# Attention and a gated MLP on one core: products taken bank by bank, low halves of the weights in eight 256-KB slots

## The chip, the core and the metric

The kernel runs on one core of a Trainium2 chip. The metric is the device time of one execution in microseconds. Engines are named as in the profile: PE (TensorE), DVE (VectorE), ACT (ScalarE), POOL (GpSimd) and SP, whose queue issues every DMA.

## What is computed

Banded attention with sinks over 4 batches of 8 heads, 768 positions of 64 columns, then a gated MLP over the 3072 tokens that come out:

```python
keep = is_sink | in_window                      # 4 sinks, a window of 128
a = softmax(where(keep, q @ k.T / 8, -1e9))
x = (a @ v).transpose(0, 2, 1, 3).reshape(3072, 512)
gate = 1.0 / (1.0 + np.exp(-(x @ w_gate)))      # 512 x 1536
val = x @ w_val                                 # 512 x 1536
out = gate * val @ w_out                        # 1536 x 512
```

The weights come as 64-bit floats and are decoded on the chip.

## The kernel before

**Work.** The tokens are twelve groups of 256 (tn 0 to 11, three per batch). `attend` makes one unit of attention, a head of a group. `CHUNKS` joins the groups to nine chunks for the MLP: 0 to 4 and 8 are one group each, 5 to 7 are pairs of two. d_ff is cut into NF = 12 slices f of 128. For each chunk and slice the MLP multiplies the transposed x by the slice's gate and value columns into PSUM banks m0 and m1 (`B_m` = 2), forms (1 + tanh) * value in `th` with `cv` as a side store, splits it into gh and gl, and multiplies by the slice's rows of w_out into output banks (the downs).

**Precision.** From chunk 1 on every product is three fp32r matmuls: high half by high, high by low, low by high. `product` is one such product of two 128-row steps, six matmuls of 256 columns. High halves of the weights stay in SBUF (`ws`, 68 slots), low halves are written to `wlo_d` in DRAM (`spare`) and streamed back for each chunk and slice by `fetch`. Chunk 0 runs in plain fp32 (`feed_whole`).

**Plain chunks** (`feed_plain`): the value matrix had the gate matrix subtracted in its first half (`halves`), so a slice is four products, all in one bank: g0, v0, v2, then g2 on top of g0; a copy of g0's part in between and an addition afterwards make the value. 24 matmuls of 256 columns and 6 of 512.

**Pairs** (`feed_pair`) use seven products instead of eight for two groups, with sums of x made by `second_half` and of the weights by `thirds`: 42 matmuls of 256 columns and 12 of 512 per slice. Two of the four output banks come from the tag "a", of which attention has the rest (`B_a` = 3; o0, o1 and o2 are banks of their own).

**Order.** `Plan` gets every operation with a priority, the engines that may take it, what it reads and writes (a tile, or one part of it) and a duration, runs a list schedule over them with modelled times, and emits the instructions in the order that comes out; each engine then keeps that order. Attention ranks by its unit number ahead of the MLP's PE work (10000 + chunk), while the MLP's ACT and DVE work ranks first (-1000 + chunk). What waits for what on the chip is set by the framework below, from the tiles that an instruction touches. Where PE has nothing early on, the plan puts a warm-up matmul (`warm`) into its order.

**Loads.** Pieces of `wlo_d` go into three slots of 512 KB (`wst`, shared with the decoding of the weights, in pool p2) and two of 256 KB (`wol`). A pair's slice loads two of 512 KB and one of 256, a plain slice one of each.

Of the kernel before, what the change touches and what calls it, by code (L numbers as in the profile page):

```python
# [24 lines left out]
CHUNKS = ((0,), (1,), (2,), (3,), (4,), (5, 6), (7, 8), (9, 10), (11,))  # L25
NWS = 68
# [7 lines left out]
HALVED = 30000.0  # L34
CROWDED = 350000.0
# [10 lines left out]
KS1 = 14.0  # L46
# [32 lines left out]
B_wol = 2  # L79
B_w2 = 2  # L80
B_wst = 3
B_a = 3
# [14 lines left out]
def general(ctx, tc, qk, v, ident, nsk, win, wres, wlo_d, out):  # L97
# [34 lines left out]
    with tc.For_i(0, B, 1) as b:  # L132
# [65 lines left out]
        with tc.For_i(0, NT, 1) as t:  # L198
# [18 lines left out]
            for f in range(NF):  # L217
                wgh, wvh, woh = wres[f]
                lows = []
                for i, n in ((1, "g"), (2, "v"), (4, "o")):  # L220
# [6 lines left out]
                for nm in "gv":  # L227
                    m = ps.tile([128, 128], F32, name="m" + nm)
                    ms.append(m)
                    g, v2 = (wgh, wgl), (wvh, wvl)  # L230
                    terms = (
                        [(c, g) for c in range(NC)] if nm == "g"
                        else [(c, g) for c in range(NC // 2)] + [(c, v2) for c in range(NC)]
                    )
                    todo = [
                        (c, w, x) for c, (wh, wl) in terms
                        for w, x in ((wh, xh), (wh, xl), (wl, xh))
                    ]
# [60 lines left out]
class Op:  # L299
    def __init__(self, prio, ways, dma, busy):  # L300
        self.prio, self.ways, self.dma, self.busy = prio, ways, dma, busy
        self.after, self.before, self.tiles = [], 0, []
# [3 lines left out]
class Plan:  # L306
# [9 lines left out]
    def op(self, prio, ways, r=(), w=(), dma=0.0, busy=0.97, start=0.0):  # L316
        o = Op(prio, ways, dma, busy)
        o.ready = start
        seen = set()
# [21 lines left out]
    def run(self, warm, fill_ns, fill):  # L341
# [35 lines left out]
        while events:  # L377
# [25 lines left out]
            for e in free:  # L403
# [4 lines left out]
                while waiting[e] or unsure:  # L408
# [66 lines left out]
                    heapq.heappush(events, (end, n, ("end", o, e)))  # L475
                    for x in o.after:
# [25 lines left out]
def kernel(  # L502
# [31 lines left out]
    p2 = main.enter_context(tc.tile_pool(name="p2", bufs=1))  # L534
    ps = main.enter_context(tc.tile_pool(name="ps", bufs=1, space=PSUM))

# [35 lines left out]
    def dma(prio, ns, fn, r=(), w=(), start=0.0):  # L572
        plan.op(prio, [("Q", ISSUE, fn)], r, w, dma=ns, start=start)
# [158 lines left out]
    idle = ps.tile([128, 512], F32, tag="o20", name="idle")  # L732
    PE.matmul(idle[:, 0:128], lhsT=ident, rhs=ident, start=True, stop=True)

    def warm():
        PE.matmul(
            idle[:, 0:128], lhsT=ident, rhs=ident, start=False, stop=True,
# [11 lines left out]
    pair_of = {x: len(parts) > 1 for parts in CHUNKS for x in parts}  # L749
# [17 lines left out]
    WLO, LOADS, GROUPS, DECODED, READY = (Fixed(None) for _ in range(5))  # L767

    def sinks(b, u):
# [21 lines left out]
        for o in range(0, 128, NS):  # L791
# [3 lines left out]
                ), [], [(raw, o)] + [VSHL[b, i] for i in range(2) if (b, i) in VSHL],  # L795
            )
        for i in range(0 if b else 1, 2):
# [3 lines left out]
            copy(u, H // 2 * D, hi, x, [raw], [both])  # L801
# [18 lines left out]
    def attend(u, b, h, t0, T, XR):  # L820
# [296 lines left out]
        if y:  # L1117
# [8 lines left out]
            elif not pair_of[tn]:  # L1126
                if c % 2 == 0:
                    for x in XH, XL:
                        x[tn, c // 2] = tile([128, 2, W], F32R, "ws", NWS, wp)
                H1, L1 = XH[tn, c // 2], XL[tn, c // 2]  # L1130
                hi, lo = lambda: H1()[:, c % 2], lambda: L1()[:, c % 2]
                copy(u, W, hi, xv, read, [(H1, c)], plain)
                rest(u, W, lo, xv, hi, read + [(H1, c)], [(L1, c)], plain)
# [7 lines left out]
    def minus(p, cols, out, a, b, r, w, add=False):  # L1141
# [7 lines left out]
            ], r, w,  # L1149
# [24 lines left out]
    wlo_d = dram.tile([NF, 128, 5 * 512], F32, name="wlo_d")  # L1174
# [79 lines left out]
    def halves(f):  # L1254
# [3 lines left out]
        woh = halve(pr, f, 4, (1, DO), wout, (), HALVED)  # L1258
        minus(
            pr, 256, lambda: value()[:, 0:2], lambda: value()[:, 0:2], lambda: gate()[:, 0:2],  # L1260
            [gate], [value],
        )
        gh = halve(pr, f, 1, (NC, 128), gate)
        vh = halve(pr, f, 2, (NC, 128), value)
        wres[f] = [gh, vh, woh]

    def thirds(f):
# [3 lines left out]
        t2 = lambda: value()[:, 2:4]  # L1271
        minus(pr, 256, t2, t2, lambda: value()[:, 0:2], [], [value])
        minus(pr, 256, lambda: gate()[:, 0:2], t2, lambda: gate()[:, 0:2], [value], [gate])
        minus(pr, 256, lambda: gate()[:, 2:4], lambda: gate()[:, 2:4], t2, [value], [gate])
        both = slot(F32R, (NC, 128))
        copy(pr, 256, lambda: both()[:, 0:2], t2, [value], [(both, 0)])
        rest(pr, 256, lambda: both()[:, 2:4], t2, lambda: both()[:, 0:2], [value, (both, 0)], [(both, 1)])
        spare(pr, f, 0, both)
        wres[f].append(halve(pr, f, 3, (NC, 128), gate))
# [15 lines left out]
    def feed(ci):  # L1295
# [4 lines left out]
            tile([128, DO], F32, f"o{j}", 1, ps) if j < 3  # L1300
            else tile([128, DO], F32, "a", BUFS["a"], ps) for j in range(T)
        ]
        for f in range(NF):
# [3 lines left out]
            elif T == 2:  # L1307
                feed_plain(ci, tcs[0], f, O)
# [55 lines left out]
    def fetch(pr, f, k, n, chain, gate=()):  # L1364
        x = (
            tile([128, n * 512], F32R, "wst", BUFS["wst"], p2) if n > 1
            else tile([128, 512], F32R, "wol", BUFS["wol"])
        )
        dma(
            pr, 728.0 * n, lambda: Q.dma_start(  # L1370
                out=x().bitcast(F32), in_=wlo_d[f, :, k * 512 : (k + n) * 512]
            ), [(WLO, (f, k + i)) for i in range(n)] + list(gate), [x, (LOADS, chain)],
        )
        return x

    def product(p, m, reg, w, c0, w2, d0, X, first, last, w_):

        XHn, XLn = X

        def go():  # L1380
            for i in range(2):
                hi, lo = w(c0 + i), w2(d0 + i)
                for k, (a, x) in enumerate(((hi, XHn), (hi, XLn), (lo, XHn))):
                    PE.matmul(
                        m()[:, reg * 256 : reg * 256 + 256], lhsT=a, rhs=x()[:, i],
# [4 lines left out]
        plan.op(p, [("PE", 6 * mac(256), go)], w_[0] + [XHn, XLn], w_[1])  # L1390

    def gated(pr, W, th, cv, step):

        gh = tile([128, W], F32R, "gh", BUFS["gh"])
        gl = tile([128, W], F32R, "gl", BUFS["gl"])
        n = W // 256
        t, c = (lambda x=x: x()[:, 0:n].rearrange("p n x -> p (n x)") for x in (th, cv))
        plan.op(
            pr, [("V", vec(W), lambda: V.scalar_tensor_tensor(
                out=t(), in0=t(), scalar=1.0, in1=c(), op0=ALU.add, op1=ALU.mult  # L1400
            ))],
            [cv], [th],
        )
# [22 lines left out]
    def feed_plain(ci, n, f, O):  # L1426
        pr = -1000.0 + ci + f / NF
        pe = 10000.0 + ci + f / NF
        gh_, vh_, woh = wres[f][:3]
        e = fetch(pr, f, 1, 2, 0, [DECODED] if ci == WHOLE else ())  # L1430
        wol = fetch(pr, f, 4, 1, 1, [DECODED] if ci == WHOLE else ())
        m = Tile(MS, None, F32, "m", BUFS["m"])
        th = tile([128, 2, 256], F32, "th", BUFS["th"])
        cv = tile([128, 2, 256], F32, "cv", BUFS["cv"])
        A1, A2 = (XH[n, 0], XL[n, 0]), (XH[n, 1], XL[n, 1])
        gw, vw = (lambda i: gh_()[:, i]), (lambda i: vh_()[:, i])
        product(pe, m, 0, gw, 0, four(e), 0, A1, True, False, ([gh_, e], [m, GROUPS]))
# [172 lines left out]
```

## Time and profile before

| | us |
|---|---|
| median of 3 runs | 856.19 (855.15 to 857.5) |
| the profiled execution | 857.94 |
| its span, first to last instruction | 855.8 |
| PE busy | 787.8 (92%), 5110 matmuls |
| DVE busy | 656.1 (77%) |
| POOL busy | 527.6 (62%) |
| ACT busy | 442.8 (52%) |
| DMA | 172.97 MB, queue 1 at 65.9% of the 16 engines |

The granted clock of PE is 0.989 over the span. The waits in the profile are the idle time of an engine just ahead of an instruction, put down to what released it. Chunk 0 ends near 157 us, chunk 4 near 434, the pairs near 565, 690 and 794; the last scores of attention are done at 704 us.

### The profile page before, as it was taken

What the parts mean: (1) busy time and instruction counts of PE and PEld (TensorE: products, weight loads), DVE (VectorE), ACT (ScalarE), POOL (GpSimd) and SP (SyncE); (2) the same over time, 40 slices, a digit from 0 to 9 for tenths busy, and PEclk for the clock granted to TensorE, in tenths of its full rate; (3) what the DMA queues carried; (4) which work ended last, traced back from release to release, by engine and by line L of the source; (5) the groups of instructions that cost most, each with busy time, mean ns of one, the idle gap of its engine ahead of it and who ended that gap; (6) DMA issues with size and microseconds to landing.
All of it is one profiled execution on the core that took longest, in us unless ns stands there. A gap on an engine that the chain in (4) does not pass through costs nothing. (4 is left out here: it accounts for less than half of the span.)

```text
span 855.8 us, 16414 instructions
## 1 busy us (share of the span) xinstructions
PE 787.8 (92%) x5110; PEld 697.1 (81%) x5110; DVE 656.1 (77%) x1871; ACT 442.8 (52%) x1288; POOL 527.6 (62%) x698
## 2 busy tenths in 40 slices
PE   7999988887999999999899999999999899999995
PEld 6777766786888898889788889898888788888884
DVE  6899999898798988738888988878887986444221
ACT  7788776552566666626565554454545661001111
POOL 4899897675667786627778678657675872111111
PEclk9999999899999999999999999999999999999998
DMA  6889887788776676667666656666665554545651
GB/s 175 230 258 294 287 261 233 235 292 286 222 224 194 205 237 181 203 201 225 185 194 192 182 169 192 184 221 194 196 194 177 142 179 139 162 148 162 196 178 55
DMA packets 111341, 172.97 MB, mean 202 GB/s; under 512 B 46480, under 2 KB 58768, under 8 KB 111248
## 3 DMA queue, kind: packets, MB, share of 16 engines
q1 hardware_dynamic: 111248, 171.86, 65.9%
q8 instruction: 43, 0.70, 0.3%
q14 instruction: 50, 0.41, 0.2%
HBM read 149.80 MB, written 22.02 MB: 201 GB/s over the span
## 5 line engine op out<-in xcount | busy, mean ns | idle before, releaser
L554 PE MATMUL m<-ws,ws 128*128 128x256 f32 x1824 | 353.8, 290 | 38.8 <-DVE cv L554 29.3
L554 PEld LDWEIGHTS m<-ws,ws 128*128 128x128 f32 x1824 | 286.3, 190 | 64.9 <-DVE cv L554 45.0
L554 PE MATMUL m<-ws,wst 128*128 128x256 f32 x1128 | 286.1, 283 | 2.4 <-DVE cv L554 1.4
L554 PEld LDWEIGHTS m<-ws,wst 128*128 128x128 f32 x1128 | 200.3, 190 | 4.1 <-ACT cv L554 1.9
L554 POOL TENSOR_TENSOR gl<-th,gh 128x256 fp32r<-128x256 f32 (+1 forms) x60 | 58.9, 982 | 142.6 <-DVE gh L554 77.3
L554 POOL TENSOR_SCALAR_AFFINE_SELECT wt<-wt 128x512 fp32r<-128x512 f32 (+3 forms) x192 | 122.7, 639 | 35.8 <-DVE wt L554 23.8
L554 DVE TENSOR_TENSOR cv<-m,cv 128x256 f32<-128x256 f32 x204 | 85.7, 420 | 65.1 <-PE m L554 58.3
L554 ACT ACTIVATE th<-m 128x256 f32<-128x256 f32 x108 | 41.6, 385 | 148.6 <-PE m L554 110.3
L554 PE MATMUL o<-ws,gh 128*128 128x512 f32 x228 | 91.9, 403 | 0.9 <-ACT w L554 0.5
L554 ACT ACTIVATE P<-P,negm_all 128x144 f32<-128x144 f32 x192 | 79.0, 412 | 23.9 <-DVE negm_all L554 22.2
L554 PE MATMUL o<-ws,gl 128*128 128x512 f32 x228 | 89.7, 394 | 0.2 <-POOLq L1564 0.2
L554 PE MATMUL o<-wol,gh 128*128 128x512 f32 x228 | 89.3, 392 | 0.0
L554 DVE SCALAR_TENSOR_TENSOR th<-th,cv 128x256 f32<-128x256 f32 (+1 forms) x96 | 61.8, 644 | 28.2 <-ACT th L554 26.0
L554 POOL TENSOR_TENSOR ws<-ws,ws 128x512 fp32r<-128x512 f32 (+2 forms) x54 | 66.2, 1239 | 12.4 <-DVE ws L554 3.5
L554 PE MATMUL a<-wt,vhl 128*128 128x256 f32 (+2 forms) x282 | 61.2, 328 | 2.8 <-DVE negm_all L554 2.2
L554 DVE CUSTOM_DVE_ANT_0 P<-a,am 128x144 f32<-128x144 f32 x192 | 58.6, 305 | 6.5 <-PE a L554 0.3
L554 POOL TENSOR_TENSOR hi<-qkT,hi 64x256 fp32r<-64x256 f32 x61 | 48.2, 790 | 16.6 <-issue 5.0
L554 PEld LDWEIGHTS a<-wt,vhl 128*128 128x128 f32 x282 | 48.1, 192 | 9.8 <-issue 2.9
L554 POOL TENSOR_TENSOR kl<-qkT,hi 128x400 fp32r<-128x400 f32 (+1 forms) x48 | 50.8, 1058 | 2.1
L554 PEld LDWEIGHTS o<-ws,gl 128*128 128x128 f32 x228 | 42.9, 188 | 10.7 <-POOLq L1564 0.6
L554 POOL TENSOR_TENSOR sk<-turned,own 128x256 fp32r<-128x256 f32 x46 | 31.4, 683 | 28.2 <-DVE turned L554 19.3
L554 ACT CAST hi<-qkT 128x656 fp32r<-128x656 f32 (+1 forms) x59 | 41.3, 701 | 13.3 <-PE a L554 12.0
(141 smaller groups left out, 1647.5 us busy)
## 6 DMA issues: line engine op xcount, KB each, us to landing
wst<-wlo_d SPq DMA_DIRECT2D x132, 512.0 KB, 3.8
wol<-wlo_d SPq DMA_DIRECT2D x96, 256.0 KB, 3.6
qkT<-in_qk_dram SPq DMA_DIRECT2D x52, 328.0 KB, 3.9
wlo_d<-ws SPq DMA_DIRECT2D x60, 256.0 KB, 3.8
qkT<-in_qk_dram SPq DMA_DIRECT2D x24, 264.0 KB, 3.4
wst<-in_moe_w_gate_dram SPq DMA_DIRECT2D x12, 512.0 KB, 5.1
wst<-in_moe_w_val_dram SPq DMA_DIRECT2D x12, 512.0 KB, 5.0
wst<-in_moe_w_out_dram SPq DMA_DIRECT2D x12, 512.0 KB, 5.0
```

The lines of the kernel that those rows point to most:

```text
L554: return lambda *a, **kw: tc.keep_in_program_order(op(*a, **kw))
```

## The change

A pair's seven products are ordered so that both halves of one bank are written in turn before the other bank is, and every reader is declared to read the whole bank. Plain chunks take the unmodified gate and value matrices: four products, gate into one bank, value into the other, no copy and no addition. The subtraction of the gate moves from `halves` to `thirds`, and `thirds` starts no earlier than 250 us. Low halves come as pieces of 256 KB in eight slots `lo` (a new pool, opened when p2 has been closed) and are issued in one chain. o2 goes, and attention's tag "a" has four banks. The warm-up matmul writes into a corner of m0.

```diff
-KS1 = 14.0
+KS1 = 16.0
+THIRDS = 250000.0
-B_wol = 2
+B_lo = 8
-B_a = 3
+B_a = 4
...
-    idle = ps.tile([128, 512], F32, tag="o20", name="idle")
-    PE.matmul(idle[:, 0:128], lhsT=ident, rhs=ident, start=True, stop=True)
+    PE.matmul(MS[0][:, 384:512], lhsT=ident, rhs=ident, start=True, stop=True)
...
-    wlo_d = dram.tile([NF, 128, 5 * 512], F32, name="wlo_d")
+    wlo_d = dram.tile([NF, 128, 6 * 512], F32, name="wlo_d")
...
     def halves(f):
-        woh = halve(pr, f, 4, (1, DO), wout, (), HALVED)
-        minus(
-            pr, 256, lambda: value()[:, 0:2], lambda: value()[:, 0:2], lambda: gate()[:, 0:2],
-            [gate], [value],
-        )
-        gh = halve(pr, f, 1, (NC, 128), gate)
-        vh = halve(pr, f, 2, (NC, 128), value)
+        woh = halve(pr, f, 5, (1, DO), wout, (), HALVED)
+        gh = halve(pr, f, 3, (NC, 128), gate)
+        vh = halve(pr, f, 4, (NC, 128), value)
...
     def thirds(f):
+        minus(pr, 256, t1, t1, g1, [gate], [value], start=THIRDS + 5000.0 * f)
+        minus(pr, 256, t2, t2, t1, [], [value])
+        minus(pr, 256, g1, t2, g1, [value], [gate])
+        minus(pr, 256, g2, g2, t2, [value], [gate])
+        hi = halve(pr, f, 1, (NC, 128), value)
+        spare(pr, f, 0, hi)
+        wres[f].append(halve(pr, f, 2, (NC, 128), gate))
...
-            tile([128, DO], F32, f"o{j}", 1, ps) if j < 3
+            tile([128, DO], F32, f"o{j}", 1, ps) if j < 2
...
+    def fetch(pr, f, *parts):
+        got = []
+        for k in parts:
+            x = tile([128, 512], F32R, "lo", BUFS["lo"], p3)
+            LAST[0] = dma(
+                pr, 728.0, lambda x=x, k=k: Q.dma_start(
+                    out=x().bitcast(F32), in_=wlo_d[f, :, k * 512 : k * 512 + 512]
+                ), [(WLO, (f, k)), DECODED], [x], behind=LAST[0],
+            )
+            got.append(x)
+        return got
...
     def feed_plain(ci, tcs, f, O):
+        glo, vlo, wol = fetch(pr, f, 3, 4, 5)
+        for i, (hi, lo) in enumerate(((gh_, glo), (vh_, vlo))):
+            m = Tile(MS, None, F32, "m", BUFS["m"])
+            for j in range(2):
+                product(
+                    pe + 0.3 * i / NF, m, 0, W, w, 2 * j, four(lo), 2 * j, cols(j), j == 0, j == 1,
+                    [hi, lo] + both(j), [m] if j else [m, GROUPS] + ([th] if i == 0 else []),
+                )
...
     def feed_pair(ci, tcs, f, O):
-        e = fetch(pr, f, 0, 2, 0)
-        l = fetch(pr, f, 2, 2, 0)
-        wol = fetch(pr, f, 4, 1, 1)
+        t12h, t12l, glo, tlo, vlo, wol = fetch(pr, f, 0, 1, 3, 2, 4, 5)
...
+        product(pe, ma, 0, 256, gw, 0, four(glo), 0, X(n, 0), True, False, [gh_, glo] + xs(n, 0), [ma, GROUPS])
         product(
+            pe + 0.05 / NF, ma, 1, 256, four(t12h), 2, four(t12l), 2, X(k, "s2"), False, True,
...
+            pe + 0.2 / NF, mb, 0, 256, tw, 0, four(tlo), 0, X(k, "s3"), True, False, [th_, tlo] + xs(k, "s3"),
...
+            pe + 0.25 / NF, mb, 1, 256, four(t12h), 0, four(t12l), 0, X(k, "s1"), False, False,
...
+            pe + 0.4 / NF, ma, 0, 256, gw, 2, four(glo), 2, X(n, 1), False, True, [gh_, glo] + xs(n, 1), [ma],
...
+            pe + 0.45 / NF, ma, 1, 256, tw, 2, four(tlo), 2, X(k, 1), True, True,
...
+            pe + 0.6 / NF, mb, 1, 256, vw, 2, four(vlo), 2, X(k, "s4"), False, True,
...
+        downs(pe, f, O, gh, gl, woh, wol, (1.3, 1.5, 1.65, 1.7))
```

PE's order in the third pair, where no attention is left. m_89 and m_90 are the two banks, ws the resident halves and sums of x, wst and lo the streamed pieces. Before, from the end of a slice's second product to the start of the fourth:

```order
L554 MATMUL m_89<-ws_9393,wst_10569 128x256
L554 MATMUL m_90<-ws_9398,ws_2447 128x256 [waits DVE_49]
L554 MATMUL m_90<-ws_9425,ws_2447 128x256
L554 MATMUL m_90<-ws_9398,wst_10606 128x256 [waits DMAHW1_49]
L554 MATMUL m_90<-ws_9398,ws_2447 128x256
L554 MATMUL m_90<-ws_9425,ws_2447 128x256
L554 MATMUL m_90<-ws_9398,wst_10606 128x256
L554 MATMUL m_89<-ws_8477,ws_1562 128x256 [waits DVE_49]
```

Between two writes of bank m_89 with a reader in between stands one product in the other bank. The same place after the change, the last matmul of the third product, the fourth, one down and the first of the fifth:

```order
L575 MATMUL m_90<-ws_9645,lo_10622 128x256
L575 MATMUL m_90<-ws_9649,lo_10575 128x256
L575 MATMUL m_90<-ws_9688,lo_10575 128x256
L575 MATMUL m_90<-ws_9649,lo_10603 128x256
L575 MATMUL m_90<-ws_9649,lo_10575 128x256
L575 MATMUL m_90<-ws_9688,lo_10575 128x256
L575 MATMUL m_90<-ws_9649,lo_10603 128x256
L575 MATMUL o_9985<-ws_1346,gh_10654 128x512 [waits DVE_49]
L575 MATMUL o_9985<-lo_10560,gh_10654 128x512 [waits DMAHW0_49]
L575 MATMUL o_9985<-ws_1346,gl_10664 128x512 [waits Pool_49]
L575 MATMUL m_89<-ws_8418,ws_1561 128x256 [waits DVE_49]
```

The third and fourth products both go to m_90, and with the down they stand between the second product and the next write of m_89.

PE's order in the last chunk, a plain one. Before, the second product of a slice and the start of its third, all in one bank:

```order
L554 MATMUL m_90<-ws_9589,ws_1080 128x256
L554 MATMUL m_90<-ws_9611,ws_1080 128x256
L554 MATMUL m_90<-ws_9589,wst_10853 128x256
L554 MATMUL m_90<-ws_9589,ws_1080 128x256
L554 MATMUL m_90<-ws_9611,ws_1080 128x256
L554 MATMUL m_90<-ws_9589,wst_10853 128x256
L554 MATMUL m_90<-ws_9995,ws_1080 128x256 [waits DVE_49]
```

The third product waits for DVE with nothing in between. After the change, the end of a slice's value product, the downs of the slice before and the start of the next gate product:

```order
L575 MATMUL m_90<-ws_10014,lo_11193 128x256
L575 MATMUL o_10976<-ws_1196,gh_11269 128x512 [waits DVE_49]
L575 MATMUL o_10976<-lo_11166,gh_11269 128x512 [waits DMAHW6_49]
L575 MATMUL o_10976<-ws_1196,gl_11271 128x512 [waits Pool_49]
L575 MATMUL o_10983<-ws_1196,gh_11269 128x512
L575 MATMUL o_10983<-lo_11166,gh_11269 128x512
L575 MATMUL o_10983<-ws_1196,gl_11271 128x512
L575 MATMUL m_89<-ws_9686,ws_1561 128x256 [waits Activation_49]
```

The gate's bank is written again after the whole value product and the downs.

SP's order in the third pair, before and after, some one and a half slices each:

```order
L554 DMA wst_10372<-wlo_d 128x1024 [waits DMAHW3_49,PE_49]
L554 DMA wst_10405<-wlo_d 128x1024 [waits DMAHW5_49,PE_49]
L554 DMA wol_10409<-wlo_d 128x512 [waits DMAHW4_49,PE_49]
L554 DMA wst_10447<-wlo_d 128x1024 [waits DMAHW6_49,PE_49]
L554 DMA wol_10482<-wlo_d 128x512 [waits DMAHW7_49,PE_49]
```

```order
L575 DMA lo_10603<-wlo_d 128x512 [waits DMAHW3_49,DMAHW2_49,PE_49]
L575 DMA lo_10608<-wlo_d 128x512 [waits DMAHW4_49,PE_49]
L575 DMA lo_10622<-wlo_d 128x512 [waits DMAHW5_49,PE_49]
L575 DMA lo_10627<-wlo_d 128x512 [waits DMAHW6_49,PE_49]
L575 DMA lo_10641<-wlo_d 128x512 [waits DMAHW7_49,PE_49]
L575 DMA lo_10656<-wlo_d 128x512 [waits PE_49]
```

Each load waits for PE's last use of its slot; a slice has six of them where it had three.

## Rows read from the trace of the kernel before

**Rows 1.** Busy time by stage: PE, PEld, DVE, ACT, POOL, clock, DMA share, GB/s
```profile
0.00:139.00 139.00, 124.63 (x619) 96.19 (x620) 126.45 (x325) 107.25 (x260) 112.72 (x135) 0.99 0.82 246
139.00:226.00 87.00, 73.54 (x478) 65.05 (x478) 73.95 (x172) 42.13 (x121) 57.14 (x71) 0.96 0.80 259
226.00:434.00 208.00, 197.68 (x1366) 181.29 (x1366) 168.10 (x547) 123.44 (x400) 139.08 (x204) 0.99 0.69 206
434.00:690.00 256.00, 241.96 (x1660) 220.46 (x1659) 218.15 (x654) 139.23 (x427) 183.00 (x244) 1.00 0.64 191
690.00:794.00 104.00, 100.16 (x674) 90.85 (x674) 54.65 (x141) 22.36 (x65) 27.66 (x37) 1.00 0.51 156
794.00:855.80 61.80, 49.84 (x324) 43.23 (x322) 14.78 (x36) 8.37 (x21) 8.04 (x11) 0.96 0.43 137
```

**Rows 2.** Timeline of PE in the third pair: start, duration, instruction, idle before
```profile
737.14 0.41 PE L554 MATMUL m<-ws,ws 128*128 128x256 f32 x2
737.38 0.28 PE L554 MATMUL m<-ws,wst 128*128 128x256 f32 x1
737.92 0.51 PE L554 MATMUL m<-ws,ws 128*128 128x256 f32 x2 [0.26 <-DVE cv L554]
...
739.47 0.40 PE L554 MATMUL o<-ws,gh 128*128 128x512 f32 x1
...
740.16 0.39 PE L554 MATMUL o<-ws,gh 128*128 128x512 f32 x1
...
746.22 0.51 PE L554 MATMUL m<-ws,ws 128*128 128x256 f32 x2 [0.26 <-DVE cv L554]
```

**Rows 3.** Timeline of DVE at the same place
```profile
736.99 0.42 DVE L554 COPY cv<-m 128x256 f32<-128x256 f32 x1 [0.59 <-PE m L554]
737.44 0.95 DVE L554 TENSOR_TENSOR cv<-m,cv 128x256 f32<-128x256 f32 x2
```

**Rows 4.** Waits of PE's products by the five stages from 139 us, in turn
```profile
PE m L554 <- DVE cv L554: 7.4, 7, 2.5
PE m L554 <- ACT cv L554: 3.7, 4, 1.6
...
PE m L554 <- DVE cv L554: 6.1, 11, 1.3
PE m L554 <- ACT cv L554: 1.8, 6, 0.5
...
PE m L554 <- DVE cv L554: 10.3, 16, 1.6
PE m L554 <- DVE th L554: 2.7, 5, 1.0
PE m L554 <- ACT cv L554: 1.0, 4, 0.4
...
PE m L554 <- DVE cv L554: 3.3, 10, 0.5
...
PE m L554 <- DVE cv L554: 4.1, 8, 0.5
```

**Rows 5.** Timeline of PE in the last chunk
```profile
797.84 0.28 PE L554 MATMUL m<-ws,wst 128*128 128x256 f32 x1
798.63 0.50 PE L554 MATMUL m<-ws,ws 128*128 128x256 f32 x2 [0.52 <-DVE cv L554]
```

**Rows 6.** Landing of wol: first from 712 to 790 us, then from 139 to 226
```profile
DMA to landing us min/median/max: 2.6/3.3/3.8
...
DMA to landing us min/median/max: 2.8/4.4/5.5
```

**Rows 7.** Chunks 2 to 4: the steps from products to a down
```profile
L554 DVE SCALAR_TENSOR_TENSOR th<-th,cv 128x256 f32<-128x256 f32 x35 | 21.4, 612 | 9.6 <-ACT th L554 9.1
...
L554 ACT CAST gh<-th x23: 389/406/411, 236.4 to 428.5; 128x256 fp32r<-128x256 f32 x23
L554 POOL TENSOR_TENSOR gl<-th,gh x16: 729/737/800, 264.8 to 406.1; 128x256 fp32r<-128x256 f32 x16
```

More of the change, by code (lines that the diff above doesn't have):

```diff
@@ L301, in __init__ @@
         self.prio, self.ways, self.dma, self.busy = prio, ways, dma, busy
-        self.after, self.before, self.tiles = [], 0, []
+        self.after, self.before, self.tiles, self.then = [], 0, [], []
         self.ready = self.sure = self.due = 0.0
@@ L314, in __init__, with op @@
         self.ops = []
-    def op(self, prio, ways, r=(), w=(), dma=0.0, busy=0.97, start=0.0):
+    def op(self, prio, ways, r=(), w=(), dma=0.0, busy=0.97, start=0.0, behind=None):
         o = Op(prio, ways, dma, busy)
         o.ready = start
+        if behind is not None:
+            behind.then.append(o)
+            o.before += 1
         seen = set()
@@ L475, in run @@
                     heapq.heappush(events, (end, n, ("end", o, e)))
+                    for x in o.then:
+                        x.before -= 1
+                        x.todo -= 1
+                        x.ready = max(x.ready, now + ns)
+                        if not x.before:
+                            n += 1
+                            heapq.heappush(events, (x.ready, n, ("ready", x, None)))
                     for x in o.after:
@@ L794, in sinks @@
                     out=raw()[o : o + NS], in_=v[b, :, 0:NS, :].rearrange("h p d -> p h d"),
-                ), [], [(raw, o)] + [VSHL[b, i] for i in range(2) if (b, i) in VSHL],
+                ), [READY2], [(raw, o)] + [VSHL[b, i] for i in range(2) if b and (b, i) in VSHL],
             )
@@ L1126, in attend @@
             elif not pair_of[tn]:
-                if c % 2 == 0:
-                    for x in XH, XL:
[L1129 to L1133, printed above, removed]
+                ci = chunk_of[tn]
+                half, wide = CHUNKS[ci].index(tn), len(CHUNKS[ci]) > 1
+                key = ("s", ci, c if wide else c // 2)
+                i = half if wide else c % 2
+                if i == 0:
+                    for x in XH, XL:
+                        x[key] = tile([128, 2, W], F32R, "ws", NWS, wp)
+                H1, L1 = XH[key], XL[key]
+                hi, lo = lambda: H1()[:, i], lambda: L1()[:, i]
+                copy(u, W, hi, xv, read, [(H1, i)], plain)
+                rest(u, W, lo, xv, hi, read + [(H1, i)], [(L1, i)], plain)
     def parts(n, j, x, p, r=()):
@@ L1139, in parts, with minus @@
         rest(p, 512, L1, x, H1, [x, H1], [L1])
-    def minus(p, cols, out, a, b, r, w, add=False):
+    def minus(p, cols, out, a, b, r, w, add=False, start=0.0):
         plan.op(
@@ L1270, in thirds @@
         gate, value, _ = wraw[f]
[L1271 to L1279, printed above, removed]
+        t1, t2 = (lambda i=i: value()[:, i : i + 2] for i in (0, 2))
+        g1, g2 = (lambda i=i: gate()[:, i : i + 2] for i in (0, 2))
+        minus(pr, 256, t1, t1, g1, [gate], [value], start=THIRDS + 5000.0 * f)
[5 more added lines that the diff above has]
+        wres[f].append(halve(pr, f, 2, (NC, 128), gate))
         if f == NF - 1:
@@ L1362, in feed_whole, with product @@
             plan.op(pe + 0.5 / NF, [("PE", 4 * DO / 2.4 + 6, down)], [th, woh], [O[j]])
[L1364 to L1378, printed above, removed]
+    def fetch(pr, f, *parts):
[9 more added lines that the diff above has]
+        return got
+    def product(p, m, reg, W, w, c0, w2, d0, X, first, last, r, w_):
         def go():
@@ L1457, in feed_pair @@
+        gh, gl = gated(pr, W, th)
+        downs(pe, f, O, gh, gl, woh, wol, (0.5,) * len(O))
     def feed_pair(ci, tcs, f, O):
```

170 lines of the change are left out of this document (92 added, 78 removed).

## Prediction

> **What bounds the kernel now.** I read the table by stage first, then the waits of TensorE in the same stretches, and last the timeline where nothing but matmuls runs. The stage table [rows 1] shows TensorE busy for 197.68 of 208 us while chunks 2 to 4 run, 241.96 of 256 in the first two pairs and 100.16 of 104 in the third: from 226 us on it is the engine that sets the end. Busy time hides what I look for, because the record of a 256-column matmul lasts 0.28 us while the next one starts 0.12 us after it [rows 2]. So I go by starts. VectorE comes next: 168.10 us of 208 and 218.15 of 256 [rows 1]. Before 139 us it is VectorE that is fullest, 126.45 of 139 us.
>
> The third pair runs without attention after 704 us and repeats every 8.30 us per slice of d_ff: the same matmul starts at 737.92 and at 746.22 [rows 2]. In between there is one stop. The last matmul of the third product starts at 737.38 and the first of the next product should follow at 737.50; it starts at 737.92, released by VectorE's write of cv. VectorE's rows say why [rows 3]. The copy out of the first product begins only at 736.99, when the second product, which writes the other half of the same bank, has ended. The wait is by bank, although the planner had planned it by half. The copy (0.42 us) and an addition (half of the 0.95 us row of two) then run while TensorE has only the third product to do, six matmuls or 0.7 us.
>
> A stop costs more than its gap. The page counts 0.26 us; the start is late by 737.92 - 737.38 - 0.12 = 0.42 us; and the first two matmuls behind it take 0.51 us where two in the stream take 0.41 [rows 2]. So a stop costs its gap plus 0.16 plus 0.10, some 0.26 us. A plain slice has the same stop in another form: the third product follows the second in one bank while a copy of the first is due, and its start is 0.79 us behind its predecessor's instead of 0.12 [rows 5].
>
> **What those stops are worth.** The waits "PE m" for cv or th, by stage [rows 4], gap and count, each with 0.26 us per stop:
> - 139 to 226 us: 7.4 + 3.7 us in 11 stops, 14.0 us
> - 226 to 434: 6.1 + 1.8 in 17, 12.3 us
> - 434 to 690: 10.3 + 2.7 + 1.0 in 25, 20.5 us
> - 690 to 794: 3.3 in 10, 5.9 us
> - 794 to the end: 4.1 in 8, 6.2 us
>
> The sum is 58.9 us.
>
> **The change, part by part.**
> *Products by bank.* The matmuls are the same in number and size: 42 and 12 per pair slice, 24 and 6 per plain slice. In a pair slice, four products of the two banks now come in twos, and the bank that is read next is left alone for two products and one down projection. The down's three matmuls take 740.16 - 739.47 = 0.69 us [rows 2], so the cover is 0.7 + 0.7 + 0.69 = 2.1 us against a copy and an addition of some 0.9 us and their two handovers, where it was 0.7 us. In a plain slice the gate fills one bank and the value the other; a bank rests for a whole 12-matmul product, 1.4 us, before it is written again, and is read by one instruction. Over the whole order, 282 products wait for a reader of their bank before and 226 after; with less than two products' matmuls in between there are 114 before and 3 after. I take three quarters of each stage off: 10 + 9 + 15 us up to 690, and nearly all of the last two, 5.5 + 5.5, where the order is the same in every slice. That is 45 us. One quarter stays, because the readers on VectorE and ScalarE queue behind attention's work.
>
> *Plain products.* A copy and an addition per plain slice go, 60 of each, and the scalar_tensor_tensor reads the bank itself. VectorE and ScalarE lose them beside TensorE; I count nothing for it.
>
> *Weights.* The subtraction of the gate from the value moves from halves to thirds, the count stays at four per slice. The third matrix is now stored as two full pieces instead of one half-and-half piece, so its copy and its remainder double. All of thirds starts no earlier than 250 us. It ran beside chunk 0 and 1 and now runs beside chunks 2 and 3, where VectorE is busy for 168.10 of 208 us [rows 1]. In that stretch VectorE loses some 20 us of copies and additions and gains about as much; cover is there, but it is VectorE's. I charge 3 us for it and credit 3 us at the start, where VectorE is fullest.
>
> *Loads.* Per pair slice six pieces of 256 KB instead of two of 512 and one of 256, 1.5 MB instead of 1.25; per plain slice three of 256 KB, the same bytes. All take turns in eight slots, each is issued behind the one before, and SP issues 396 (60 slices by three, 36 by six) where it issued 228. What stands behind a waiting load on SP are attention's loads of qkT and v. The shortest time between the last use of a slot and the first use of the next piece in it is, at TensorE's pace, 5.1 us in the pure pair stage (down, two products, down, product, two downs, two matmuls). A load needs 3.3 us (median of 256 KB in that stage, 3.8 at most) [rows 6], and about 0.7 for its issue behind another and the handovers. It fits with 0.6 us to spare, so nothing; the upper bound is the 5.5 us that one took between 139 and 226 us [rows 6], 1.1 us late, on 36 slices 40 us.
>
> The Trainium skill ("DMA: Bandwidth & Descriptors", on the anatomy of one DMA) speaks against small pieces: about 2.0 us fixed plus the bytes at 436 GB/s, half efficient at some 860 KB. By it a 256-KB piece takes an estimated 2.6 us, the six of a slice 15.6; two at a time that is 7.8 us per slice, and the sum would be some 3 us worse. The fastest load in the trace did take 2.6 us; but the rule prices one load alone, and here up to eight are under way.
>
> *Four attention banks, p3, the warm-up bank.* Two of the four hold outputs during a pair, so a pair leaves attention two, as before; plain chunks leave four instead of three. The fourth only helps. The warm-up matmuls now write a bank that chunk 0 uses; most of them stand ahead of chunk 0. Nothing for all three.
>
> *Downs closer to their products.* A plain slice's down now comes two to three products after the value product, where it was mostly more than four us of matmuls. The chain in between is the scalar_tensor_tensor (0.61 us), the cast (0.41) and the remainder on POOL (0.74) [rows 7], 1.8 us and four handovers: it just fits when the engines are free, less so beside attention. I charge 3.5 us.
>
> **The sum.** 45 + 3 - 3 - 3.5 = 41.5 us off the profiled execution's 857.94 us (its span is 855.8). That run lies 1.75 us above the median of the three runs, 856.19, so I forecast 856.2 - 41.5 = **815 us**.
>
> **The rivals.**
> *VectorE becomes the bound.* From 226 to 690 us it is busy for 386 of 464 us [rows 1], 83%, and its work hardly falls. If its share can't rise above 85%, those 464 us can't fall below 455, which gives 9 us of the 24 taken there; with 10, 5.5 and 5.5 from the other stages and the 3.5 charge, 26 us: 830. For it: attention's chain has to be answered in order. Against it: the first 139 us show VectorE at 91%.
>
> *The wait moves to the downs.* If gl comes 0.6 us late in 48 plain slices beside attention, 29 us of the gain are lost instead of 3.5: 841. For it: three engines take part in the chain, and POOL is at 139 of 208 us [rows 1]. Against it: in the trace downs wait for next to nothing, and the planner lets a ready product go first.
>
> *Loads come late, and the kernel is slower.* Place: the first product of a pair slice and the loads queued behind on SP. It decides from a landing of 4.4 us on (5.1 less 0.7). At 5.5 us all 36 slices lose 1.1 us, 40 us; and each piece that waits at the head of SP's queue holds attention's loads, which in the 24 slices beside attention I price at as much again, 26 us. Against the gain of 41.5 that is 857 + 24 = 881 at worst; with half of the slices at the full price and attention held in all, 861. For it: 256-KB loads had a median of 4.4 us where the DMA share was 0.80 [rows 1, 6]. Against it: the pairs ran at 0.64 and 0.51, and 20% more bytes don't bring them to 0.80.
>
> *The change doesn't reach the stops.* If VectorE and not the bank were late, the products would wait as before: 856. The copy that began only when the second product had ended speaks against it.
>
> **How the numbers follow.** The forecast gets 0.64, VectorE's bound 0.13, the downs 0.12, no effect 0.04, late loads 0.07. If all 58.9 us go and the start gains its 3, the time is 794; that is the lower end. The upper end, 846, takes in the downs' and VectorE's cases with some margin, and leaves out no effect and late loads. Some 0.3% is what a measurement of this kernel can tell from no change. Faster: 0.64 + 0.13 + 0.12 = 0.89; same 0.04; slower 0.07.
>
> **What would show it.** Right: in the pure pair stage a slice takes 7.7 to 7.8 us (8.30 less the 0.42 and the restart), the last chunk 4.2 us per slice, and the waits of "PE m" for cv and th shrink to a quarter. VectorE's share from chunk 2 to the second pair is about 0.9. Wrong: TensorE's waits name a load of lo, or gl and gh, with ten us or more; or matmuls of the attention wait for VectorE. If the time is above 846, the covers in the order were not what mattered.

## The result, and the profile after

The changed kernel takes **808.32 us** (median of 4 runs, 807.94 to 808.95) against 856.43 (855.15 to 857.5) for the kernel before: ratio 0.944, 95% interval 0.9423 to 0.9456. The forecast was 815 in a range of 794 to 846. The profiled execution has a span of 807.2 us, 48.6 less than before.

The stage table of the kernel after, cut where the same work ends (first column the stretch, then its length, then PE, PEld, DVE, ACT, POOL busy, clock, DMA share, GB/s), answers to [rows 1]:

```profile
139.00:207.00 68.00, 65.22 (x455) 59.46 (x454) 46.57 (x145) 33.72 (x103) 42.68 (x60) 1.00 0.83 267
207.00:408.00 201.00, 194.15 (x1361) 178.63 (x1361) 184.29 (x531) 125.73 (x389) 152.15 (x212) 1.00 0.81 253
408.00:657.00 249.00, 241.42 (x1663) 219.67 (x1662) 235.51 (x676) 147.82 (x452) 183.07 (x240) 1.00 0.71 221
657.00:751.00 94.00, 94.00 (x653) 87.62 (x652) 43.43 (x102) 17.81 (x49) 19.96 (x21) 1.00 0.66 207
```

Chunk 1 now ends at 207 us instead of 226. VectorE is busy for 95% of the first two pairs (235.51 of 249), where it was 85%.

TensorE's waits in the five stages of the kernel after (total, times, longest). From 139 to 207 us:

```profile
PE a L575 <- DVE wt L575: 1.3, 1, 1.3
PE o L575 <- DVE th L575: 0.9, 1, 0.9
PE m L575 <- DVE th L575: 0.4, 1, 0.4
```

From 207 to 408 us:

```profile
PE m L575 <- DVE th L575: 2.5, 5, 0.6
...
PE o L575 <- DVE gl L575: 0.7, 1, 0.7
...
PE o L575 <- DVE gh L575: 0.4, 1, 0.4
...
PE o L575 <- ACT w L575: 0.2, 1, 0.2
```

From 408 to 657 us:

```profile
PE a L575 <- DVE xf L575: 2.3, 3, 1.4
PE a L575 <- DVE negm_all L575: 1.9, 3, 0.8
PE m L575 <- DVE cv L575: 1.3, 3, 0.9
PE a L575 <- DVE wt L575: 0.7, 3, 0.3
PE m L575 <- DMA lo<-wlo_d: 0.6, 1, 0.6
PE a L575 <- POOL P L575: 0.3, 1, 0.3
```

From 657 to 751 us nothing is listed. From 751 us on:

```profile
PE o L575 <- DVE total L1606: 0.8, 1, 0.8
```

The stops of "PE m" on cv and th, 40.4 us in 71 stops before [rows 4], are 4.2 us in 9. New are the waits of attention's matmuls ("PE a") in the pairs, 5.2 us in 10; before, that stage listed none.

The timeline of PE in the third pair, one slice apart, and in the last chunk, two slices apart:

```profile
716.84 0.40 PE L575 MATMUL o<-ws,gh 128*128 128x512 f32 x1
...
724.62 0.40 PE L575 MATMUL o<-ws,gh 128*128 128x512 f32 x1
...
769.81 0.40 PE L575 MATMUL o<-ws,gh 128*128 128x512 f32 x1
...
778.29 0.40 PE L575 MATMUL o<-ws,gh 128*128 128x512 f32 x1
```

A pair slice repeats every 7.78 us (8.30 before, [rows 2]), a plain slice every (778.29 - 769.81) / 2 = 4.24. VectorE now has time between a bank's two products and its next write:

```profile
717.09 0.42 DVE L575 TENSOR_TENSOR th<-m,cv 128x256 f32<-128x256 f32 x1 [0.67 <-PE m L575]
717.55 0.42 DVE L575 TENSOR_TENSOR cv<-m,th 128x256 f32<-128x256 f32 x1
719.16 0.42 DVE L575 TENSOR_TENSOR th<-m,th 128x256 f32<-128x256 f32 x1 [1.19 <-PE m L575]
```

It waits for the products now, and TensorE doesn't wait for it.

### The profile page after: what moved, and what is told of

It reads as the page before. It is cut to its first block, busy times and chain, and to the rows that moved or that the text cites. A ratio compares the mean times of both kernels' runs of the same rounds, so it can differ in the third digit from the quotient of the medians.

```text
span 807.2 us, 16573 instructions
## 1 busy us (share of the span) xinstructions
PE 767.6 (95%) x5084; PEld 686.2 (85%) x5084; DVE 636.8 (79%) x1806; ACT 440.6 (55%) x1258; POOL 508.3 (63%) x675
## 5 line engine op out<-in xcount | busy, mean ns | idle before, releaser
L575 PE MATMUL m<-ws,ws 128*128 128x256 f32 x1680 | 316.1, 285 | 4.3 <-DVE th L575 2.9
L575 PE MATMUL m<-ws,lo 128*128 128x256 f32 x1272 | 293.1, 282 | 1.3 <-POOL ws L575 0.7
L575 PEld LDWEIGHTS m<-ws,ws 128*128 128x128 f32 x1680 | 265.6, 189 | 16.1 <-DVE th L575 4.2
L575 PEld LDWEIGHTS m<-ws,lo 128*128 128x128 f32 x1272 | 212.4, 189 | 2.2 <-DMA lo<-wlo_d 1.0
L575 ACT ACTIVATE th<-m 128x256 f32<-128x256 f32 x108 | 41.5, 384 | 127.7 <-PE m L575 78.9
L575 DVE SCALAR_TENSOR_TENSOR th<-th,m 128x256 f32<-128x256 f32 x72 | 29.8, 414 | 64.3 <-PE m L575 63.2
L575 PE MATMUL o<-lo,gh 128*128 128x512 f32 x192 | 75.1, 391 | 0.0
L575 POOL TENSOR_TENSOR ws<-ws,ws 128x512 fp32r<-128x512 f32 (+1 forms) x47 | 60.7, 1298 | 6.9 <-ACT ws L575 2.6
L575 POOL TENSOR_TENSOR hi<-qkT,hi 64x256 fp32r<-64x256 f32 x60 | 49.9, 832 | 15.7 <-issue 5.6
L575 PE MATMUL a<-ident,P 128*128 128x128 f32 (+1 forms) x212 | 40.4, 277 | 9.9 <-POOL P L575 3.3
L575 DVE TENSOR_TENSOR cv<-m,cv 128x256 f32<-128x256 f32 x72 | 30.0, 417 | 24.8 <-ACT cv L575 14.7
L575 PE MATMUL a<-hi 128*128 128x272 f32 (+1 forms) x152 | 44.8, 305 | 3.0 <-DVE negm_all L575 1.1
```

Of the source, the lines that this page charges most:

```text
L575: return lambda *a, **kw: tc.keep_in_program_order(op(*a, **kw))
```

## The experiments

The time that each chunk adds, from the end of the last down of one to that of the next, in the profiled execution; the medians stand beside it. By this cut chunk 0 ends at 142 us before and after; the 157 us given above for the kernel before is where its first output is stored.

| run | median us | chunk 1 | 2 to 4 | pairs 1, 2 | pair 3 | last |
|---|---|---|---|---|---|---|
| before | 856.4 | 84.0 | 207.3 | 255.3 | 103.3 | 56.7 |
| after | 808.3 | 65.1 | 200.5 | 249.2 | 94.0 | 49.6 |
| before, thirds late | 869.0 | 70.6 | 206.5 | 280.1 | 106.1 | 55.2 |
| before, planned by bank | 870.9 | 82.6 | 205.3 | 285.6 | 99.9 | 51.2 |
| after, pair's old order | 824.9 | 64.5 | 202.2 | 254.2 | 101.7 | 49.6 |
| after, plain slices old | 850.6 | 71.4 | 240.1 | 235.6 | 96.8 | 59.0 |
| after, plain extra work | 816.6 | 66.2 | 218.5 | 237.2 | 93.9 | 49.9 |
| after, DVE work in pairs 1, 2 | 806.0 | 64.9 | 200.6 | 245.7 | 94.6 | 49.6 |
| after, DVE work in pair 3 | 808.6 | 64.7 | 201.1 | 251.6 | 94.0 | 49.6 |
| after, thirds from 160 us | 803.6 | 63.8 | 207.1 | 240.6 | 93.8 | 49.6 |
| after, thirds from 180 us | 804.1 | 62.9 | 199.9 | 246.8 | 97.1 | 49.6 |
| the same, plain extra work | 809.7 | 64.4 | 195.7 | 252.7 | 97.1 | 49.9 |
| the same, plain slices old | 843.6 | 72.2 | 207.1 | 260.8 | 96.3 | 58.6 |
| after, thirds from 160 us, 3 apart | 801.4 | 67.4 | 199.5 | 242.0 | 94.4 | 49.6 |

Each row is one execution, and each edit goes through the plan again, which then also orders other operations anew and gives some of them to other engines. Additions in pair 3 alone moved the first two pairs, which they don't touch, by 2.4 us. A difference of that size in one column proves nothing.

### One part alone: thirds late

```diff
 (before)
+THIRDS = 250000.0
-        minus(pr, 256, t2, t2, lambda: value()[:, 0:2], [], [value])
+        minus(pr, 256, t2, t2, lambda: value()[:, 0:2], [], [value], start=THIRDS + 5000.0 * f)
```

> The kernel before, with the third matrix of the weights made from 250 us on instead of as early as it can be. Theory A: the 20 us that the changed kernel has gained by the end of chunk 1 come mostly from this move, because VectorE no longer has that work beside chunks 0 and 1; then chunk 1 ends at 212 to 216 us here instead of 226, chunks 2 to 4 take as long or a little longer, and the time is 844 to 852. Theory B: they come from the plain products; then chunk 1 ends at 222 us or later and the time is 854 to 862.

869.04 us, ratio 1.0137 (1.0093 to 1.0181): by itself this part costs time, which neither theory had. Chunk 1 is shorter by 13.4 us, as theory A said (it ends at 213 us), but the first two pairs take 24.8 more. The stage rows show how (columns as above):

```profile
380.00:390.00 10.00, 9.48 (x67) 8.53 (x67) 3.04 (x10) 1.36 (x4) 1.74 (x3) 1.00 0.73 218
390.00:400.00 10.00, 9.48 (x68) 8.65 (x67) 4.58 (x12) 2.58 (x7) 3.18 (x5) 1.00 0.50 150
420.00:430.00 10.00, 5.40 (x23) 3.98 (x22) 9.48 (x39) 7.29 (x24) 6.95 (x13) 0.79 0.67 199
430.00:440.00 10.00, 5.53 (x20) 4.21 (x19) 9.83 (x24) 6.93 (x20) 8.99 (x9) 0.50 0.06 13
```

At 380 us TensorE works through the MLP while VectorE is nearly idle; when chunk 4 is done at 419 us, the next pair's tokens have not come out of attention, VectorE is full, TensorE half empty, and its granted clock is at the lower level (0.50, 1.2 GHz) for ten microseconds. Why attention did not go on at 380 us, with VectorE free, is not shown.

### One part alone: the plan knows the banks

The readers are declared as reading the whole bank; the pair's first copy moves behind the second product; the order of the products stays.

```diff
 (before)
-            [(m, 0)], [th],
+            [m], [th],
...
-                [(m, i)] + r, w,
+                [m] + r, w,
```

> The kernel before with the same products, loads, weights and PSUM banks; only the declarations to the plan are by bank instead of by half, with the first copy of a pair slice moved behind its second product, so that the plan knows of the waits. Products with under 1.25 us of matmuls between two writes of a bank fall from 114 to 77. Theory A: the stops come from the order of the products itself, which this keeps inside a slice; where nothing else is left to put in between (third pair, last chunk) they stay, beside attention some 15 of 47 us go: 838 to 848. Theory B: the plan's ignorance was the whole cause: 815 to 825.

870.88 us, ratio 1.0141 (1.0098 to 1.0185); both theories missed it. The last chunk gains 5.5 us and pair 3 gains 3.4, the first two pairs lose 30.3 (the profiled execution, at 876.29, lies 5.4 above the median). TensorE's waits in them:

```profile
PE m L554 <- DVE cv L554: 17.7, 23, 2.2
PE a L554 <- DVE negm_all L554: 2.5, 5, 1.0
PE a L554 <- DVE wt L554: 2.5, 5, 1.3
```

In this order of the products, knowing the banks doesn't remove the stops beside attention. The next run puts back the order and the declarations together, and the stops return.

### The pair's order undone

Products, readers and downs of the pair as before, all else as after.

```diff
 (after)
-        product(pe + 0.25 / NF, mb, 1, ...)
+        product(pe + 0.15 / NF, ma, 0, ...)
+        product(pe + 0.2 / NF, mb, 1, ...)
...
-                [m] + r, w,
+                [part] + r, w,
```

> The changed kernel with a pair's seven products in the order and with the declarations of before; loads, weights, plain chunks and banks stay as changed. Products with under 1.25 us between two writes of a bank rise from 3 to 75, all in the three pairs. Theory A: the stops come back in the pairs: 8.3 us per slice in the third pair instead of 7.9, and 10 to 15 us in the first two: 822 to 830. Theory B: VectorE sets the pace of the first two pairs, so that only the third gets longer, by 5 us: 811 to 815.

824.92 us, 16.6 more than after; its profiled execution, 822.06, shows 13.2 us more span. The total is theory A's 822 to 830, the first two pairs give less than it said: pair 3 takes 7.7 more and they together 5.0. Their stops are back (third pair last):

```profile
PE m L575 <- DVE cv L575: 7.5, 14, 1.1
PE m L575 <- DVE th L575: 2.0, 5, 0.8
PE m L575 <- ACT cv L575: 1.4, 5, 0.4
...
PE m L575 <- DVE cv L575: 2.0, 8, 0.3
```

### The plain slices undone, and only their work given back

```diff
 (after; first run: the four products, copy and addition of before in one bank)
-        for i, (hi, lo) in enumerate(((gh_, glo), (vh_, vlo))):
-            m = Tile(MS, None, F32, "m", BUFS["m"])
+        m = Tile(MS, None, F32, "m", BUFS["m"])
...
 (after; second run: the new order, with work added)
+                copy(pr, 256, lambda: cv()[:, 0], lambda m=m: m()[:, 0:256], [m], [cv], True)
...
+                        out=cv()[:, 0], in0=m()[:, 0:256], in1=cv()[:, 0], op=ALU.add
```

> The kernel after, with its plain slices alone put back: one bank for gate and value, the old order of the four products, the copy of the gate's first half and the addition (the value is left without the gate's subtraction, so this run adds the gate's first half to it and computes another function). Theory A (plain slices paid for stops by bank, and for nothing else): chunk 1 grows from 65.1 us by the 5.5 that the late thirds leave unexplained, to about 71; chunks 2 to 4 grow by 2 to 3 us each; the last chunk returns from 49.6 to 55 to 57 us; the pairs stay within 3 us of those of after; total 821 to 830 us. Theory B (what counted was VectorE and ScalarE, which lose a copy and an addition per plain slice and can keep attention up): the last chunk grows by less than 2 us, but attention falls behind beside chunks 1 to 4 and the first pair takes 145 us or more where after has 127.9, as with the late thirds alone; total 830 to 850 us. Both can hold: then the last chunk and the first pair both grow.

> The kernel after with its order of products kept, and in each plain slice the copy of the gate's bank and an addition from the value's bank as extra work whose result nobody reads (60 of each, 0.42 us apiece). Theory A (the stops count, the relief doesn't): no chunk more than 2 us longer, total 808 to 812 us. Theory B (the relief of VectorE and ScalarE counts): chunks 2 to 4 together and the first pair take 10 us or more longer, the last chunk, which has no attention beside it, stays at 49.6; total 820 us or more.

850.63 and 816.61 us. The first loses 42.3 us of the gain of 48: chunk 1 grows as theory A said (6.3), the last chunk by more than it said (9.4, to 59.0 where it had 55 to 57), but chunk 4 takes 31.9 us more. The second grows by 8.3 us, with 24.6 more in chunk 4 and 10.3 less in the first pair. Both have one stall in chunk 4, of 14.1 and 14.3 us. The timelines of PE and of ACT in the second run, its waits there and its DMA from 330 to 365 us:

```profile
343.09 0.28 PE L575 MATMUL m<-ws,lo 128*128 128x256 f32 x1
357.69 0.80 PE L575 MATMUL o<-ws,gh 128*128 128x512 f32 x1 [14.31 <-ACT w L575]
```

```profile
348.09 0.62 ACT L575 CAST ws<-ws 128x512 fp32r<-128x512 f32 x1 [1.96 <-DMA wlo_d<-ws]
350.73 1.27 ACT L575 CAST ws<-ws 128x512 fp32r<-128x512 f32 x2 [2.02 <-DMA wlo_d<-ws]
...
357.04 0.60 ACT L575 ACTIVATE w<-o 128x512 f32<-128x512 f32 x1 [2.66 <-DVE own L575]
```

```profile
PE o L575 <- ACT w L575: 15.1, 2, 14.3
...
ACT ws L575 <- DMA wlo_d<-ws: 8.1, 7, 2.0
```

```profile
DMA packets 7510, 12.81 MB, mean 366 GB/s; under 512 B 1364, under 2 KB 1364, under 8 KB 7509
...
wlo_d<-ws SPq DMA_DIRECT2D x35, 256.0 KB, 4.1
lo<-wlo_d SPq DMA_DIRECT2D x10, 256.0 KB, 4.6
```

The thirds, allowed from 250 us on, had bunched up: 35 stores in 35 us, 22 of them in a row in SP's written order. ScalarE's casts wait for slots that the stores hold, the copy of an output bank stands behind them in ScalarE's order (and waits for VectorE 2.66 us more), and TensorE's next down waits for that bank. So both runs say more of the thirds than of the plain slices. They were repeated with thirds that start early enough to spread.

### The thirds spread, then the same two again

```diff
 (after)
-THIRDS = 250000.0
+THIRDS = 180000.0
```

> The kernel after with the thirds allowed from 180 us on instead of 250 (still 5 us apart per slice). In the written order of SP no more than two of their stores now follow each other without a load of lo between them; in the kernel after up to three, in the run with extra work in the plain slices 22. Theory A (late thirds bunch up: their stores fill the DMA engines and their casts hold VectorE and ScalarE in order, so TensorE stops in lumps): chunks 2 to 4 lose the stops that after shows between 280 and 340 us, where TensorE was busy for 55.3 of 60 us, and the first pair starts with attention further ahead; total 797 to 803 us, no wait of TensorE over 3 us from 208 us on. Theory B (the 803.6 us of the start at 160 us was an accident of the order): 803 to 812 us.

> The run before this one, with the copy and the addition per plain slice as extra work whose result nobody reads, as in the earlier run of that kind, whose stores came 22 in a row beside a stall of 14.3 us. Here no more than two stores follow each other. Theory A (the relief of VectorE and ScalarE counts for little, the stall was the bunch of stores): within 4 us of the run with thirds from 180 us and nothing added, last chunk 49.6 to 50 us. Theory B (the relief counts): 8 us or more above it.

> The plain slices in their old form and order as in the earlier undoing (one bank, copy and addition; the gate's first half is added to the value, so another function is computed), with the thirds from 180 us on, their stores at most two in a row. Theory A (what plain slices paid were stops by bank, and the 32 us that chunk 4 gained in the earlier run were the bunch of stores): against the run with thirds from 180 us alone, chunk 1 takes 6 us more, chunks 2 to 4 take 2 to 4 us more each, the last chunk 7 to 9.5 us more; total 18 to 28 us more, no stall over 5 us. Theory B (the old form itself stops TensorE beside attention): again 35 us or more, with a wait of over 10 us in one piece.

804.14 us (ratio 0.938, 0.9341 to 0.9418), 809.70 (0.9459, 0.9444 to 0.9475) and 843.57 (0.986, 0.9843 to 0.9877). The first lies outside theory A's 797 to 803, by 1 us, and inside theory B's; so it doesn't decide between them. It has one wait of 3.3 us, for a load of lo at 414 us. Giving the work back costs 5.6 us, between the two theories. Undoing the plain slices costs 39.4 us, which is theory B's 35 or more and not theory A's 18 to 28; but the stall that B wanted is gone, the longest wait is 4.0 us. Chunk 1 takes 9.3 more, where A had 6; chunks 2 to 4 take 7.2 more and the last chunk 9.0, as A had them; and the first two pairs take 14.0 more, which it had not. TensorE's waits from 139 to 418 us in that run:

```profile
PE m L575 <- ACT cv L575: 11.3, 23, 2.0
PE m L575 <- DVE cv L575: 9.1, 15, 1.6
```

38 stops, 20.4 us, where the run with the new form has 3.6 us in 5 on th. Attention's matmuls stand in the same queue, so each stop makes attention late too; its last scores come at 690 us instead of 663. I take that to be the 14.0 us in the pairs; no run parts it from the rest. The start of the first pair agrees with it: there TensorE stands half idle and its granted clock falls (it was busy for 16.26 of the first 20 us of that pair in the run with the new form):

```profile
420.00:430.00 10.00, 4.50 (x16) 3.53 (x17) 9.87 (x20) 7.41 (x21) 8.33 (x10) 0.65 0.35 116
430.00:440.00 10.00, 8.73 (x57) 8.04 (x57) 9.80 (x35) 6.38 (x22) 9.01 (x13) 0.84 0.63 186
```

### VectorE's share tested

```diff
 (after; first run in pairs 1 and 2, second run twice per slice in pair 3)
+                plan.op(
+                    pr, [("V", vec(256), lambda: V.tensor_tensor(
+                        out=cv()[:, 0], in0=th()[:, 0], in1=th()[:, 1], op=ALU.add
+                    ))],
+                    [th], [cv],
+                )
```

> The kernel after with one more 256-column addition on VectorE (0.42 us) in each of the 24 slices of the first two pairs, 10 us of work in all, put behind the downs; its result is overwritten unread. VectorE is busy for 118.99 of 126 and 95.45 of 100 us there. If VectorE is the bound beside attention: the two pairs take 8 to 14 us longer, total 816 to 822 us. If TensorE is still the bound there: less than 3 us, total 808 to 811 us.

> The same 10 us of additions put into the third pair, two in each of its 12 slices, where VectorE is busy for 21.67 of 78 us. Both theories: less than 1.5 us, total 807.5 to 810 us. If it costs more than 3 us, an addition there delays the chain that TensorE waits for, and the run beside it says nothing on VectorE's share.

805.95 us (ratio 0.9402, 0.9381 to 0.9424) and 808.58, neither longer than after; the first two pairs even took 3.5 us less. But the first run did not do what it was meant for. The plan, with the additions in it, gave other operations of VectorE to ScalarE and POOL (casts to gh among them). The first two pairs of the first run and the third pair of the second:

```profile
408.00:653.00 245.00, 237.40 (x1653) 218.52 (x1652) 225.20 (x658) 149.56 (x459) 181.65 (x247) 1.00 0.73 224
```

```profile
657.00:751.00 94.00, 94.00 (x653) 87.62 (x652) 49.03 (x117) 24.44 (x59) 19.73 (x21) 1.00 0.66 207
```

VectorE was busy for 225.20 of 245 us, with 24 additions more and 42 other instructions fewer than in the 235.51 of 249 us after. So its load there never rose, and whether VectorE at 95% holds the first two pairs back stays open; what the run shows is that the plan can make room for 10 us at no cost. In the third pair VectorE's load did rise, from 43.43 to 49.03 of 94 us, and cost nothing.

### Earlier thirds, for a faster kernel

```diff
 (after; first run, second run)
+THIRDS = 160000.0
...
+THIRDS = 160000.0
+        minus(pr, 256, t1, t1, g1, [gate], [value], start=THIRDS + 3000.0 * f)
```

> The changed kernel with the third matrix made from 160 us on instead of 250. VectorE is half idle from 160 to 200 us and 99% busy from 280 to 340 us, where TensorE loses 9 us. Theory A: VectorE was the bound there; those 9 us go and little comes at 160 to 220: 799 to 804. Theory B: the loss moves with the work: 806 to 811.

> The kernel after with the thirds from 160 us on and 3 us apart per slice instead of 250 and 5, so that all of them may start by 193 us; in SP's written order at most three of their stores follow each other. If an early start that spreads the thirds over chunks 1 and 2, where VectorE is busy for 11 to 12 of 20 us, is what helped at 160 and 180 us: chunks 1 to 4 together take 258 to 264 us where after takes 265.6, the pairs stay at 240 to 247 us, total 798 to 804 us. If the gains at 160 and 180 us were accidents of the order: anywhere from 803 to 812 us, with the first pair above 127 us.

803.57 us (ratio 0.9378, 0.9333 to 0.9424) and **801.36** (0.9352, 0.9322 to 0.9382). The first has a total that theory A named, but not from the place that A named: it gains 8.6 us in the first two pairs and gives 6.6 back in chunks 2 to 4. The second has an interval that lies wholly below that of the change, and the lowest median of the study, though its interval overlaps those of the starts at 160 and 180 us, 5 us apart. Its total was as expected and the place was not: chunks 1 to 4 gain nothing (266.9 us, expected 258 to 264), the first two pairs gain 7.2. Its runs spread over 797.87 to 805.67 us where those of after spread over 1 us. Why the pairs gain is open.

Not tried: other counts of lo slots, and three attention banks. What the eight slots and the fourth bank give by themselves is not shown.

## Why the prediction was nearly right, and where it was not

**Banks (right).** The wait was by bank, and it went: a pair slice takes 7.78 us (forecast 7.7 to 7.8), a plain slice 4.24 (4.2), the stops on cv and th fell from 40.4 us to 4.2, more than the three quarters I took. Undoing the pair's order costs 16.6 us, undoing the plain slices' 39.4 (the latter with the thirds from 180 us, and with the 5.6 us that the copy and addition cost by themselves). That is 56 where the whole change gave 48, so the parts don't add up: what a stop costs depends on what else is late.

**Credit for thirds at the start (wrong, too small).** I credited 3 us, before 139 us, where VectorE is fullest. There it gave nothing: chunk 0 ends at 142 us in both kernels. Chunk 1 has it: moving the thirds alone took 13.4 us off it, and the plain form gives 6.3 to 9.3 there; together about the 18.9 us that the chunk gained, where I had 10.

**Charge for thirds later (wrong in kind).** I charged 3 us beside chunks 2 and 3, and there it fits: chunks 2 to 4 gained 6.8 us where my terms, 9 less 3 less a part of the downs' charge, made 5. But the move has costs of another kind, which I left out. Alone it costs 24.8 us in the first pairs, with no more than two of its stores in a row, because attention comes late; and in two orders 22 stores in a row go with a stall of 14 us. The change shows neither, in an order where at most three stores follow each other; I had foreseen neither cost, so that it escapes both is luck. (Six in a row, in the run with thirds from 160 us, made no wait over 1.0 us in chunks 1 to 4, so a short row is not enough for a stall.) Starting the thirds at 160 us, 3 us apart, gave 7 us more.

**The first two pairs (wrong, 15 us forecast, 6.1 got).** The products' stops did go, but attention's matmuls now wait. At 0.26 us per stop above its gap, the stage had 14.0 + 25 x 0.26 = 20.5 us before [rows 4] and has 7.1 + 14 x 0.26 = 10.7 after, of which three quarters are attention's. So the stops fell by 9.8 us and the stage by 6.1. The 3.7 us between are, at least in part, work moved in: attention has 345 matmuls in the stage where it had 331, and its last scores come at 661 us, 4 us into the third pair, where they came at 704, 14 us into it.

**Pair 3 and the last chunk (5.5 each forecast, 9.3 and 7.1 got).** In pair 3, 12 x (8.30 - 7.78) = 6.2 us are the stops; the other 3 are attention's matmuls that no longer fall into it (20 of them in the stage where there were 40; in all 653 matmuls where there were 674). The last chunk lost 7.1 us against 6.2 of stops; undoing its form costs 9.0.

**Downs (right, and charged too high).** Waits of downs are 2.2 us in 4 up to 408 us, 3.2 with the price of a stop, where I charged 3.5. Only two of them, 1.1 us, are for gl and gh, the chain that I charged for; the 0.9 us for th are chunk 0's.

**Loads (right).** TensorE waits 0.6 us for lo in the first two pairs and not at all in the third:

```profile
lo<-wlo_d SPq DMA_DIRECT2D x150, 256.0 KB, 3.6
...
lo<-wlo_d SPq DMA_DIRECT2D x70, 256.0 KB, 3.2
```

The median landing, 3.6 and 3.2 us, stays under the 4.4 from which that rival decides. Eight slots did not mean eight loads under way: in the third pair 70 loads of 3.2 us in 94 us make 2.4 at a time on average, and never more than four are. A load came late once by more than 1 us, in the run with thirds from 180 us (3.3 us).

The price that I worked out from the Trainium skill ("DMA: Bandwidth & Descriptors", the anatomy of one DMA), an estimated 3 us more, doesn't show. That section gives its figures for transfers that GpSimd issues, and these loads go through SP's queue, so it did not price them directly. One load here took 3.2 us in the median, not less than the estimated 2.6, and still TensorE didn't wait.

**VectorE as the bound (didn't come as I had put it).** Its share rose to 95% where the rival had held it at 85, so the 455 us that it gave as the least for chunk 2 to the second pair became 450. Whether VectorE holds the first two pairs back at 95% is not shown; of the 7.1 us that TensorE waits there, all but the 0.6 for lo and 0.3 for POOL are for VectorE.

**The sum.** I forecast a gain of 41.5 us and the change gave 48. By stage the terms, without the charge for the downs, miss by about -3 us up to the end of chunk 0, +9 in chunk 1, +1 in chunks 2 to 4, -9 in the first two pairs, +4 in the third and +2 in the last chunk. That the two misses of 9 us cancel is luck; the mechanism, stops by bank that go with the order of the products, is not.

## What to carry to other kernels

Where two halves of a PSUM bank are tiles of one dependency, order the products so that a bank is finished before it is read and rests while the other is filled; telling the planner alone made it slower. Price a stop with what stands behind it in the same queue: the plain slices' stops cost beside attention more than their own gaps (up to the second pair 30.5 us, with 16.8 us more of gaps, in the run with thirds from 180 us). Before moving background work to a later time, look at whether its stores come in a row in the issue order, since everything behind them in the casts' queue waits too.

## What the hardware showed that I had not expected

A stall takes the clock with it. In the run with extra work in the plain slices TensorE stood for 14.3 us, and the granted clock, 1.00 before, was on average 0.71 in that stretch and 0.86 in the next, so part of both ran at the lower of its levels, 1.2 GHz:

```profile
340.00:360.00 20.00, 5.69 (x33) 4.62 (x31) 17.98 (x24) 7.46 (x14) 15.16 (x12) 0.71 1.05 397
360.00:380.00 20.00, 19.25 (x119) 17.42 (x120) 17.40 (x56) 12.86 (x42) 13.75 (x23) 0.86 0.78 235
```

The first down behind the stall took 0.80 us where one takes 0.40 in the third pair. And an experiment that adds work to an engine has to be read from the engine's busy time afterwards: VectorE was busy for 235.51 of 249 us of the first two pairs in the kernel after, and with 10 us of additions put in for 225.20 of 245 us, because the plan took other work off it.
